# A tile for each half of attention A's values, and a later load of B's output weights

## The chip, the cores and the metric

The kernel runs on one core of one Trainium2 chip. The metric is the device time of one execution in microseconds (us); lower is better. The engines are TensorE (PE, with its weight loads as PEld), VectorE (DVE), ScalarE (ACT), GpSimd (POOL) and SyncE (SP), which here issues nearly all DMAs.

## The reference, cut to what matters

Two attentions with 32 heads of 20 columns over 2048 tokens of width 640, each followed by its output weights `wo`; the results stand side by side in the output (2048 x 1280, bf16).

```python
# A: four segments of 512 tokens, causal inside a segment, plus a memory of the segments before
for s in range(4):
    p = softmax(qs @ ks.T * scale + causal_mask)
    a_dot = p @ vs
    a_mem = (phi(qs) @ M) / (phi(qs) @ z + 1e-6)
    o = g * a_mem + (1 - g) * a_dot            # g = sigmoid(beta), one for each head
    M, z = M + phi(ks).T @ vs, z + phi(ks).sum(tokens)
a = concat(o) @ A_wo
# B: a sliding window of 256 tokens
b = softmax(where(0 <= i - j < 256, q @ k.T * scale, -1e9)) @ v
b = b @ B_wo
out = concatenate([a, b], axis=-1)
```

## The kernel before

The work is cut into eight chunks of 512 tokens, taken in turn: A0, B0, A1, B1, A2, B2, A3, B3, numbered 0 to 7. The third chunk is number 2 (A1), the fifth is number 4 (A2). For each chunk PE makes q, k and v from the transposed input `xT`, the scores of four heads at a time (`score_batch`, L814), ACT takes their exponentials (L830), POOL and DVE mask them (L869, L847), PE multiplies with the values (`av`, L883), DVE transposes the sum (L949) and POOL divides it (L987). The finished chunk goes through DRAM (`scr_o`), comes back transposed as `oT`, and PE multiplies it with the output weights `wo_A` or `wo_B` (`final_job`, L935 with tiles `wo_B,oT`).

The order of the instructions is written when the kernel is built. A model of the engines (`Flow`) keeps estimated times, and a string `PLAN` fixes the order on PE: `v20` is the first half of the values of chunk 2, `o10` the output product of chunk 1, and so on. DMAs are put on SP's queue in the order of the model's times. `load_w` enters a load with a condition and a due time; the condition `known(2, "q", 3)` holds once the model has made piece 3 of q of chunk 2. SP issues in its order and each DMA waits for what it needs, and for the eighth DMA before it.

The values of A live in one tile `vA` of 128 tokens x 4 token tiles x 696 columns. Columns 0 to 347 hold heads 0 to 15 (half 0) and columns 348 to 695 heads 16 to 31 (half 1); each head has 20 columns of values and one of ones, which sums the weights, and 12 columns of ones close each half (`HV` is 348, `at_head` gives a head's column). `v_job` makes one half: for each of the four token tiles five matmuls into a PSUM bank (L935 or L930), then one multiply on DVE that writes the tile (L733) and frees the bank. When a half is done `v_squares` copies 64 of its 128 token rows by two DMAs (L757) into the tile `vS`, shifted by 64 partitions, for the ends of the causal triangles. `dm_job` uses `vA` for the memory (L686). Dependencies are kept by tile, and where two accesses to a tile with steps may meet, the later one gets a wait.

On the start, POOL fills the ones of `vA` and `vB` (`v_ones`, L796 and L800) and zeroes `vS` (L1357).

Of the kernel before, what the change touches and what calls it, by code (L numbers as in the profile page):

```python
# [13 lines left out]
P = 128  # L14
# [70 lines left out]
def at_head(h):  # L85
    return VS * h + 12 * (h // 16)
# [181 lines left out]
class _K:  # L268
# [391 lines left out]
    def dm_job(self, seg, pkT, v):  # L660


        nc, f = self.nc, self.f
        yield self.known("pkT", seg)
        W = 4 * VS
        KT = self.KT
        spare = self.pkS
        nc.gpsimd.tensor_copy(
            out=spare[:].rearrange("p k (u r) -> p (k u) r", r=HD - DH),
            in_=pkT[:].rearrange("p k (u c) -> p (k u) c", c=HD)[:, :, DH:])  # L670
        there = f.on_pool(1000.0)
        own = [(lambda kt, m=m: pkT[:, kt, P * m:P * m + P], P, [m], m) for m in range(KT)]
        for some in (own, [(lambda kt, h=h: spare[:, kt, R2 * h:R2 * h + R2], R2,
                            [x for x in range(4) if MEM2[x][0] == h], None) for h in (1, 0)]):
            if some is not own:
                yield there
            yield "bank"
            dM, bi = self.bank()
            at = 0
            for lhs, rows, xs, g0 in some:  # L680

                gs = [g0] if g0 is not None else sorted(MEM2[x][1] for x in xs)
                n = W * len(gs)
                v0 = at_head(4 * gs[0])
                for kt in range(LT):
                    nc.tensor.matmul(dM[0:rows, at:at + n], lhsT=lhs(kt),  # L686
                                     rhs=v[:, kt, v0:v0 + n],
                                     start=(kt == 0), stop=(kt == LT - 1))
                f.on_pe("full", 4 * mm_ns(n), 4 * n, 0.0, 4)
                at += n  # L690
                if (rows, xs) != (some[-1][1], some[-1][2]):
                    yield 0.0

            rows = some[0][1]
            dv = dM[0:rows, 0:at].rearrange("p (x j c) -> p x j c", j=4, c=VS)
            if rows == P:
                mz = self.mz[:, 0:KT]
            else:
                mz = self.mz[0:rows, KT:].rearrange("p (b a) j c -> p a b (j c)", a=2)
                dv = dv.rearrange("p (a b) j c -> p a b (j c)", a=2)  # L700
            nc.vector.tensor_tensor(out=mz, in0=dv, in1=mz, op=ALU.add)
            self.close(bi, f.on_dve(100.0 + 1.04 * at, f.seen))
            f.open = False
        t = f.dve + 138.0
        yield self.known(2 * seg, "avs")
        blk, mz = self.blk, self.mz
        nc.gpsimd.tensor_tensor(out=blk[:, :, :, DH], in0=mz[:, :, :, DH], in1=self.bm[:],
                                op=ALU.mult)
        f.on_pool(150.0, t)
        nc.gpsimd.tensor_tensor(out=blk[:, :, :, 0:DH], in0=mz[:, :, :, 0:DH],  # L710
                                in1=self.ez[:].unsqueeze(3)
                                .to_broadcast([P, KT + 4, 4, DH]), op=ALU.mult)
        self.mark(f.on_pool(1700.0), "dm", seg)

    def v_job(self, n, half, w_ap, v, gate, needs):
        nc, f = self.nc, self.f
        for need in needs:
            yield need
        xT = self.xs[n]
        x0 = SH if gate else 0  # L720
        for tt in range(LT):
            yield "bank"
            ps, bi = self.bank()
            for kt in range(self.KT):
                self.wide(ps, xT[:, kt, x0 + tt * P:x0 + (tt + 1) * P],
                          w_ap[:, half, kt, :], 320, kt == 0, kt == self.KT - 1)
                if kt < self.KT - 1:
                    yield 0.0
            src = ps[:, 0:320].rearrange("p (h e) -> p h e", e=DH)
            dst = v[:, tt, HV * half:HV * half + 16 * VS].rearrange(  # L730
                "p (h e) -> p h e", e=VS)[:, :, 0:DH]
            if gate:
                nc.vector.tensor_tensor(  # L733
                    out=dst, in0=src,
                    in1=self.omg[:, 16 * half:16 * half + 16].unsqueeze(2)
                    .to_broadcast([P, 16, DH]), op=ALU.mult)
            else:
                nc.vector.tensor_copy(out=dst, in_=src)  # L738
            self.close(bi, f.on_dve(402.0, f.seen))
            f.open = False  # L740
        if not gate:
            self.v_ends(n, self.chunks[n][1], half, v)
        else:
            self.v_squares(n, half, v)
        self.used_x(n)

    def v_squares(self, n, half, v):


        f = self.f  # L750
        s = slice(HV * half, HV * half + HV)
        tok = v[0:SH, :, s].rearrange("p (a b) c -> p a b c", b=2)
        t = f.dve + 138.0

        def go():
            for odd in (0, 1):
                self.nc.sync.dma_start(  # L757
                    out=self.vS[SH * odd:SH * odd + SH, odd * 2:odd * 2 + 2, s],
                    in_=tok[:, :, odd, :])
                tl = f.on_dma(1, 410.0, t) + (1200.0 if n == 0 else 0.0)  # L760
            for g in range(4 * half, 4 * half + 4):
                self.mark(tl, n, "v", g)
        f.at(t, go)

    def v_ends(self, n, c, half, v):


        f = self.f
        lo, hi = slice(0, SH), slice(SH, P)
        s = slice(HV * half, HV * half + HV)  # L770
        todo = []
        if half == 0 and c > 0:
            pv = self.vB[(c - 1) % 2]
            todo += [(self.vU[hi, 0:2, :], pv[hi, 2:4, :], 820.0),
                     (self.vX[lo, :], pv[lo, 0, :], 410.0)]
        todo += [(self.vL[lo, :, s], v[lo, :, s], 820.0),
                 (self.vU[hi, 2:4, s], v[hi, 0:2, s], 410.0),
                 (self.vX[hi, s], v[hi, 0, s], 205.0)]
        t = f.dve + 138.0

        def go():
            for out, in_, ns in todo:
                self.nc.sync.dma_start(out=out, in_=in_)
                tl = f.on_dma(1, ns, t)
            for g in range(4 * half, 4 * half + 4):
                self.mark(tl, n, "v", g)
        f.at(t, go)

    def v_tile(self, name, now=True):
        v = self.big.tile([P, LT, VW], BF16, name=name)  # L790
# [83 lines left out]
    def av(self, parts, g, vof):  # L874
        nc, f = self.nc, self.f
        O, bi = self.bank()
        parts = sorted(parts, key=lambda e: (-e[2], e[1]))
        cols = 0
        for n_, (ref, q0, nq, c0, pts) in enumerate(parts):
            v = vof(ref)  # L880
            for j in range(4):
                h = 4 * g + j
                nc.tensor.matmul(O[HD * j:HD * j + HD, q0:q0 + nq],  # L883
                                 lhsT=v[:, at_head(h):at_head(h) + HD],
                                 rhs=pts[j // 2][:, j % 2, c0:c0 + nq],
                                 start=(n_ == 0), stop=(n_ == len(parts) - 1),
                                 tile_position=(0, HD * j), skip_group_check=True)
            cols += nq
        f.on_pe("col", cols / 2.4 + 6.0 * len(parts), cols, 0.0, 4 * len(parts))
        return O, bi  # L890
# [412 lines left out]
    def body(self, xA, A_wq, A_wk, A_wv, A_wo, A_beta, xB, B_wqkv, B_wo, out2d):  # L1303
# [39 lines left out]
        self.vL = big.tile([P, LT, VW], BF16, name="vL")  # L1343
        self.vU = big.tile([P, LT, VW], BF16, name="vU")
        self.vX = big.tile([P, VW], BF16, name="vX")
        self.vA = self.v_tile("vA")
        self.vS = big.tile([P, LT, VW], BF16, name="vS")
        self.consts_mz()
        nc.vector.memset(self.vL[:].bitcast(F32), 0.0)
        for t in (self.vU, self.vX):  # L1350
# [3 lines left out]
        nc.gpsimd.memset(self.kB[0][:, :, 0:SH], 0.0)  # L1354
        nc.gpsimd.memset(self.kB[0][:, KT:G, L:XC], 0.0)
        self.consts_ends()
        nc.gpsimd.memset(self.vS[:].bitcast(F32), 0.0)  # L1357
        f.on_pool(10500.0)
        f.on_dve(4500.0)
        k = len(self.loads)  # L1360
# [8 lines left out]
                                   None, 22000.0)  # L1369
        wo = {}  # L1370
        wo["A"] = self.load_w("wo_A", A_wo, self.known(0, "scored"), 6000.0)
        wo["B"] = self.load_w("wo_B", B_wo[0], self.known(2, "q", 3), 6000.0)

        wo["end"] = self.load_w("wo_end", B_wo[1], self.known(NC - 1, "q", KT - 1), 9000.0,
                                self.wt["wk_A"][:].rearrange("p m k c -> p (m k c)").rearrange(
# [191 lines left out]
    def one_group(self, n, kind, c, g, what, parts, left, o_t, groups_done, scro, wo, out2d):  # L1567
# [3 lines left out]
        def vof(ref):  # L1571
            what, u = ref
            if what == "a":
                return self.vA[:, u, :]
            if what in "st":
                return self.vS[:, 2 * (u % 2) + u // 2, :]
            if what == "l":
                return self.vL[:, u % LT, :]
            if what == "u":
                return self.vU[:, u + 2, :]  # L1580
            if u == 0:
                return self.vX[:]
            return self.vB[c % 2][:, u, :] if u > 0 else self.vB[(c - 1) % 2][:, LT + u, :]
# [128 lines left out]
```

## Time and profile before

| what | us |
|---|---|
| median of 3 runs | 332.24 |
| lowest and highest run | 330.19, 332.38 |
| the profiled execution's own time | 332.54 |
| its span, first to last instruction | 330.7 |
| PE, ACT, POOL, DVE busy | 316.4, 299.6, 265.4, 255.8 |
| DVE's multiplies that write vA (L733), 32 | 0.48 each |
| DMAs vS<-vA (L757), 16 | 87 KB each |
| loads of wo_B (L319), 2 | 400 KB each, issued at 73.2 |
| PE's first product with wo_B | starts at 149.6 |

All times in the text are from the start of the span of the profiled execution. A queue such as SPq lists when an engine issues a DMA, not when it lands. A wait is written "engine, line, what it works on <- what ended the wait". PE's granted clock was 1.00 throughout.

### The profile page before, as it was taken

The numbers are of one execution on the slowest core, as the hardware profiler recorded it, in microseconds if no ns is written. First come the engines' busy times: TensorE is split into PE (matmuls) and PEld (weight loads), VectorE is DVE, ScalarE is ACT, GpSimd is POOL, SyncE is SP. The second block draws the span as 40 slices with busy tenths as digits, with TensorE's granted clock in tenths as the row PEclk, the third lists the DMA queues.
The fourth block names the chain that finished last, engine by engine and source line by source line (L and its number), as shares of the span: only waits on it lengthen the run. The fifth ranks groups of instructions, "written<-read, shape, count | busy, mean of one in ns | idle before, by whom it ended". The sixth has DMA issues, their size and how long they took to land.

```text
span 330.7 us, 16968 instructions
## 1 busy us (share of the span) xinstructions
PE 316.4 (96%) x7195; PEld 176.2 (53%) x7195; DVE 255.8 (77%) x533; ACT 299.6 (91%) x333; POOL 265.4 (80%) x672
## 2 busy tenths in 40 slices
PE   7999999998999999999999999999999999999984
PEld 2454546555445455646653546456654445666652
DVE  6777767797977787999867897988777798876753
ACT  1979999998999998989999999899999999979962
POOL 8466679997759899976886999998975899989850
PEclk9999999999999999999999999999999999999999
DMA  7975945675589354165689146117868027397642
GB/s 210 388 250 135 194 138 108 150 193 159 135 214 217 67 115 132 22 141 147 138 216 174 33 86 157 50 32 154 147 181 186 14 54 185 107 233 159 109 127 80
DMA packets 76266, 47.45 MB, mean 143 GB/s; under 512 B 48382, under 2 KB 73182, under 8 KB 76190
## 3 DMA queue, kind: packets, MB, share of 16 engines
q1 hardware_dynamic: 75469, 45.71, 57.7%
q8 instruction: 56, 0.92, 1.2%
q10 hardware_dynamic: 720, 0.66, 0.7%
q14 instruction: 21, 0.16, 0.2%
HBM read 17.62 MB, written 16.96 MB: 105 GB/s over the span
## 4 chain that ended last, share of the span: by engine, by line
PE 36%; DVE 5%; ACT 3%; DMA 2%; POOL 2%; issue 1%; SPq 1%; ACTq 0%; DVEq 0%
PE m L935 19%; PE sc L814 7%; PE m L883 5%; ACT pt L830 3%; PE m L930 2%; DVE tt L949 2%; PE m L904 1%; DMA xT<-scr_o 1%; DVE pt L847 1%; DMA scr_o<-o 1%; POOL pt L869 1%; DVE kA L557 1%; POOL o L987 1%; DVE ot L1099 0%; PE m L686 0%
## 5 line engine op out<-in xcount | busy, mean ns | idle before, releaser
L830 ACT ACTIVATE pt<-sc 128x1024 bf16<-128x1024 f32 (+2 forms) x306 | 282.9, 1026 | 15.1 <-PE sc L814 12.9
L869 POOL TENSOR_SCALAR_AFFINE_SELECT pt<-pt 128x128 bf16<-128x128 bf16 (+1 forms) x512 | 178.0, 376 | 49.8 <-ACT pt L830 42.8
L949 DVE STREAM_TRANSPOSE tt<-m 128x512 f32<-128x512 f32 x88 | 61.2, 709 | 24.7 <-PE m L883 15.9
L987 POOL TENSOR_TENSOR o<-tt,rr 128x320 bf16<-128x320 f32 x64 | 48.5, 758 | 4.7 <-DVE rr L977 3.9
L814 PE MATMUL sc<-qB,kB 20*64 20x64 bf16 (+2 forms) x1728 | 39.9, 217 | 0.8 <-ACT pt L830 0.3
L935 PEld LDWEIGHTS <-xT 128*128 128x128 bf16 x296 | 26.7, 97 | 18.4 <-issue 6.1
L847 DVE TENSOR_TENSOR pt<-pt,ends 128x1024 bf16<-128x1024 bf16 (+2 forms) x50 | 36.4, 739 | 0.0
L1099 DVE CAST ot<-m 128x320 bf16<-128x320 f32 x58 | 28.1, 486 | 9.8 <-PE m L935 8.4
L814 PEld LDWEIGHTS <-kB 20*64 20x64 bf16 (+1 forms) x1728 | 22.2, 98 | 22.4 <-issue 20.5
L814 PE MATMUL sc<-qA,kA 20*64 20x64 bf16 (+4 forms) x1024 | 33.5, 237 | 0.5 <-ACT pt L830 0.4
L935 PEld LDWEIGHTS <-oT 128*128 128x128 bf16 x244 | 21.5, 97 | 12.5 <-issue 3.3
L814 PEld LDWEIGHTS <-kA 20*128 20x128 bf16 (+1 forms) x1024 | 13.4, 97 | 22.4 <-issue 21.3
L935 PE MATMUL m<-wBv,xT 128*128 128x320 bf16 x147 | 24.2, 299 | 0.9 <-DVE tt L949 0.4
L883 PE MATMUL m<-pt,vA 128*32 128x192 bf16 (+3 forms) x512 | 23.6, 274 | 0.2
L935 PE MATMUL m<-wo_A,oT 128*128 128x320 bf16 x125 | 21.0, 300 | 0.8 <-DVE kA L557 0.8
L935 PE MATMUL m<-xT,wBq 128*128 128x512 bf16 x82 | 21.4, 380 | 0.3 <-DVE tt L949 0.3
L935 PE MATMUL m<-xT,wBk 128*128 128x512 bf16 x81 | 20.7, 381 | 0.0
L935 PE MATMUL m<-wv_A,xT 128*128 128x320 bf16 x119 | 20.0, 300 | 0.2 <-DVE vA L733 0.2
L738 DVE CAST vB<-m 128x320 bf16<-128x320 f32 x32 | 15.6, 488 | 5.4 <-PE m L935 3.1
L935 PE MATMUL m<-wo_B,oT 128*128 128x320 bf16 x109 | 18.6, 300 | 0.8 <-DVE tt L949 0.4
L557 DVE CAST qB<-m 128x512 bf16<-128x512 f32 x20 | 13.8, 688 | 6.7 <-PE m L930 3.4
L935 PE MATMUL m<-xT,wk_A 128*128 128x512 bf16 x69 | 17.7, 379 | 1.2 <-DMA xT<-in_A_x_dram 1.1
(127 smaller groups left out, 460.2 us busy)
## 6 DMA issues: line engine op xcount, KB each, us to landing
out_dram<-ot SPq DMA_DIRECT2D x29, 160.0 KB
scr_o<-o SPq DMA_DIRECT2D x28, 160.0 KB
xT<-in_B_x_dram SPq DMA_DIRECT2D x8, 288.0 KB
xT<-in_A_x_dram SPq DMA_DIRECT2D x8, 256.0 KB
scr_pk<-e SPq DMA_DIRECT2D x15, 128.0 KB
vS<-vA SPq DMA_DIRECT2D x16, 87.0 KB
vL<-vB SPq DMA_DIRECT2D x8, 174.0 KB
scr_kA<-kA SPq DMA_DIRECT2D x16, 60.0 KB
```

Source lines behind the costliest of these rows:

```text
L557: nc.vector.tensor_copy(out=dst[:, m, at:at + L], in_=ps[:, :])
L738: nc.vector.tensor_copy(out=dst, in_=src)
L814: nc.tensor.matmul(ps[j // 2][h0:h1, j % 2, c0:c0 + nq], lhsT=k[rows, g, k0:k0 + h1 - h0], rhs=q[rows, g, q0:q0 + nq], start=True, stop=Tr ...
L830: nc.scalar.activation(out=pt[:, :, lo:hi], in_=ps[i][:, :, lo:hi], func=ACT.Exp, scale=self.scale)
L847: nc.vector.tensor_tensor(out=blk, in0=blk, in1=self.ends[:, c0, :].unsqueeze(1).unsqueeze(1) .to_broadcast([P, 2, n // SH, SH]), op=ALU.mult)
L869: nc.gpsimd.affine_select(out=blk, in_=blk, pattern=pat, compare_op=ALU.is_ge, fill=self.zero, base=base, channel_multiplier=mul)
L883: nc.tensor.matmul(O[HD * j:HD * j + HD, q0:q0 + nq], lhsT=v[:, at_head(h):at_head(h) + HD], rhs=pts[j // 2][:, j % 2, c0:c0 + nq], start= ...
L930: self.nc.tensor.matmul(ps[s, 0:n], lhsT=lhsT[:, s], rhs=rhs, start=start, stop=stop, tile_position=(0, HD * j), skip_group_check=True)
L935: self.nc.tensor.matmul(ps[:, 0:n], lhsT=lhsT, rhs=rhs, start=start, stop=stop, skip_group_check=True)
L949: self.nc.vector.transpose(out=tt[:], in_=O[:, :])
L987: nc.gpsimd.tensor_tensor(out=to[:] if add_to else to, in0=a, in1=b, op=ALU.mult)
L1099: nc.vector.tensor_copy(out=ot[:, 320 * hf:320 * hf + 320], in_=ps[:, 0:320])
```

## The change

`vA` and `vS` become lists of two tiles, one for each half of the heads, with 348 columns each; every reader takes the tile of its half and the column inside it. The copies keep their shape. POOL fills and zeroes two smaller tiles in place of each large one. The load of `wo_B` gets a later condition: q of chunk 4 in place of q of chunk 2. On PE, ACT and DVE the order of the instructions stays the same; on POOL three memsets of `vA` become four and one of `vS` two; on SP the two loads of `wo_B` move from before the copies `vS<-vA` of half 0 of chunk 2 to behind the last input loads of chunk 5, ahead of the stores `scr_o` of chunk 3.

```diff
@@ dm_job
-                v0 = at_head(4 * gs[0])
+                v0 = at_head(4 * gs[0]) - HV * (gs[0] // 4)
...
-                                     rhs=v[:, kt, v0:v0 + n],
+                                     rhs=v[gs[0] // 4][:, kt, v0:v0 + n],
@@ v_job
-            dst = v[:, tt, HV * half:HV * half + 16 * VS].rearrange(
+            own, c0 = (v[half], 0) if gate else (v, HV * half)
+            dst = own[:, tt, c0:c0 + 16 * VS].rearrange(
@@ v_squares
-        s = slice(HV * half, HV * half + HV)
-        tok = v[0:SH, :, s].rearrange("p (a b) c -> p a b c", b=2)
+        tok = v[half][0:SH].rearrange("p (a b) c -> p a b c", b=2)
...
-                    out=self.vS[SH * odd:SH * odd + SH, odd * 2:odd * 2 + 2, s],
+                    out=self.vS[half][SH * odd:SH * odd + SH, odd * 2:odd * 2 + 2, :],
@@ new
+    def half_tiles(self, name):
+        return [self.big.tile([P, LT, HV], BF16, name="%s%d" % (name, x)) for x in range(2)]
@@ av
-                h = 4 * g + j
+                at = at_head(4 * g + j) - (HV * (g // 4) if ref[0] in "ast" else 0)
...
-                                 lhsT=v[:, at_head(h):at_head(h) + HD],
+                                 lhsT=v[:, at:at + HD],
@@ body
-        self.vA = self.v_tile("vA")
-        self.vS = big.tile([P, LT, VW], BF16, name="vS")
+        self.vA = self.half_tiles("vA")
+        for t in self.vA:
+            nc.gpsimd.memset(t[:, :, 0:16 * VS].rearrange("p t (h e) -> p t h e", e=VS)[
+                :, :, :, DH], 1.0)
+            nc.gpsimd.memset(t[:, :, HV - 12:HV], 1.0)
+        self.vS = self.half_tiles("vS")
...
-        nc.gpsimd.memset(self.vS[:].bitcast(F32), 0.0)
+        for t in self.vS:
+            nc.gpsimd.memset(t[:].bitcast(F32), 0.0)
...
-        wo["B"] = self.load_w("wo_B", B_wo[0], self.known(2, "q", 3), 6000.0)
+        wo["B"] = self.load_w("wo_B", B_wo[0], self.known(4, "q", 0), 6000.0)
@@ one_group, vof
-                return self.vA[:, u, :]
+                return self.vA[g // 4][:, u, :]
...
-                return self.vS[:, 2 * (u % 2) + u // 2, :]
+                return self.vS[g // 4][:, 2 * (u % 2) + u // 2, :]
```

## The prediction

> **What bounds the kernel now.** I read the busy shares first. TensorE (PE) is busy 96% of the span of 330.7 us and runs one fixed order of instructions, so whatever it idles in the middle of the kernel is lost; ScalarE (ACT) has 91%, VectorE (DVE) 77%.
>
> ```profile
> PE 316.4 (96%) x7195; PEld 176.2 (53%) x7195; DVE 255.8 (77%) x533; ACT 299.6 (91%) x333; POOL 265.4 (80%) x672
> ```
>
> PE therefore has 14.3 us of idle time in all. Busy time by stretches of 20 us says where: 2.0 us lie before 20 us, 5.6 us after 312 us, and the largest loss in between is 2.0 us from 72 to 92 us, in the third chunk (the second of attention A).
>
> ```profile
> 60.00:72.00 12.00, 11.99 (x277) 6.45 (x273) 10.59 (x23) 11.44 (x14) 11.86 (x28) 1.00 0.72 180
> 72.00:92.00 20.00, 18.00 (x387) 9.95 (x389) 16.93 (x39) 18.51 (x23) 14.71 (x34) 1.00 0.59 149
> ```
>
> The columns are the stretch, its length, then busy time of PE, PEld, DVE, ACT and POOL, the granted clock (1.00 throughout), the share of the DMA engines and GB/s. The waits inside that stretch name the cause:
>
> ```profile
> PEld L883 <- DVE vA L733: 1.5, 1, 1.5
> DVE vA L733 <- DMA vS<-vA: 1.5, 1, 1.5
> PE m L883 <- DVE vA L733: 1.0, 1, 1.0
> ...
> PE m L935 <- DVE kA L557: 0.8, 2, 0.5
> ...
> PE m L935 <- DVE vA L733: 0.2, 1, 0.2
> ```
>
> DVE stands for 1.5 us before one write of values (L733) because a DMA still reads that tile, and PE stands 1.0 us for DVE, then 0.8 and 0.2 us for DVE work behind it. The timelines of the three queues put times to it (start, length, engine, line):
>
> ```profile
> 71.44 1.67 SPq L651 DMA_DIRECT2D scr_pk<-e  x2
> 73.17 2.07 SPq L319 DMA_DIRECT2D wo_B<-in_B_wo_dram  x2
> 75.33 1.33 SPq L757 DMA_DIRECT2D vS<-vA  x2
> 76.75 1.76 SPq L509 DMA_DIRECT2D scr_qA<-qA  x4
> ```
>
> ```profile
> 77.51 0.52 DVE L598 TENSOR_TENSOR pq<-pq,e 128x512 bf16<-128x512 bf16 x1
> 79.51 0.49 DVE L733 TENSOR_TENSOR vA<-m,omg 128x320 bf16<-128x320 f32 x1 [1.49 <-DMA vS<-vA]
> ```
>
> ```profile
> 78.44 0.62 PE L930 MATMUL m<-xT,wk_A 128*32 128x512 bf16 x8
> 80.06 0.29 PE L883 MATMUL m<-pt,vX 128*32 128x256 bf16 x4 [1.01 <-DVE vA L733]
> ```
>
> SP issues the 800 KB of wo_B at 73.17, and the copies vS<-vA of heads 0 to 15 behind them at 75.33; they have landed when DVE goes on at 79.51. What DVE then writes is vA of heads 16 to 31, which those copies don't read: one tile holds both halves.
>
> The chain of waits from the end reaches back only to 163 us, so it doesn't itself say that this stall sets the end. I take it to do so because PE's order is fixed and, between 88 and 163 us, PE waits on no DMA at all: each of its waits there is 0.3 us or less, on DVE, ACT, POOL or issue, whose work PE itself feeds.
>
> **The change part by part.**
>
> *Two tiles for vA.* With a tile to each half, L733 for heads 16 to 31 waits for its matmul alone; the order of the instructions shows the DMA wait gone there. The matmul had ended (wv_A,xT x5 from 76.68 for 0.85 us, so 77.5), so L733 starts when DVE is free, at 78.02 instead of 79.51: 1.49 us. Walked on: PE gets its bank 1.01 us earlier (it was free at 79.05). DVE is then busy without a gap until past 85.1, so its cast kA (L557) moves from 81.18 to 79.69, after its matmul's end at 79.06; PE, which waited 0.47 us for it until 81.91, gets there at 80.43 and finds it done at 80.42. PE is now 1.48 us ahead. The waits of 0.36 us (85.15) and 0.16 us (86.15) stay, since DVE and PE moved alike. ACT idled 0.93 us at 81.0 for the same cast and 0.50 us at 86.9 for PE: it can follow by 1.43 us. POOL idled 1.32 us before 80.25 for DVE and 0.38 us at 82.5, enough to follow. I take 1.45 us. Lower bound: 1.01 us, only PE's wait on L733. Upper bound: 2.0 us, all four waits.
>
> It is the only wait of the kind that cost anything: over the whole trace the line "DVE vA L733 <- DMA" counts one. The other removed waits and their semaphore steps (21 ns each, at most 14) I cost at nothing: below 0.3 us on an engine that is 77% busy.
>
> *DVE against POOL.* In the stretch that moves, the multiply pq (L598) took 0.91 us at 80.35, beside POOL's o (L987) from 80.25 for 0.73 us, and 0.42 us at 82.80. The Trainium skill, SBUF — State Buffer, section Who interferes with whom, says that a VectorE instruction with two SBUF inputs and a GpSimd instruction that reads SBUF exclude each other, and that the one to issue second blocks. By it the 0.49 us depends on who is first: DVE would reach L598 at 78.86 and POOL its o no earlier than 78.93, so DVE would win and the gain would be some 1.9 us; were the old order kept, it stays at 1.45 us. One such pair can't settle it; the sum keeps 1.45 us.
>
> *vS as two tiles.* Still 16 copies of 87 KB with rows of the same length; no change. The reads by PE (L883, L686) keep shapes and count: no change.
>
> *POOL's fills at the start.* One memset of vA's ones (0.67 us) and two of its ends (0.51 us) become four, vS's 1.25 us becomes two halves. By the small memsets (0.10 us for one element) that adds 0.1 to 0.3 us. POOL ends them at 7.94 and idles 2.34 us until 10.28 for ACT, so nothing shows; uncovered it would be those 0.3 us.
>
> *wo_B out of the third chunk.* Two issues (2.07 us on SP) and 819 KB leave. At the 240 GB/s of 75 to 79 us those bytes are 3.4 us of transfers ahead of vS and scr_qA. SP's next instruction, vS, waits for L733 of the same half (ended 75.48), so SP gains little there. But scr_qA and the loads qA behind it (81.26) come some 1 to 2 us sooner. No PE or ACT wait in that stretch names those DMAs, so this alone is worth nothing more. It overlaps with the first part: with vS no longer behind wo_B, the copies would land some 1.5 to 3 us sooner, and most of the 1.49 us would go by this edit alone. The two gains don't add up.
>
> *wo_B into the fifth chunk.* By the order of instructions the two issues now come on SP after the loads xT of 125.39 (which end at 127.02) and before scr_o:
>
> ```profile
> 125.39 1.63 SPq L355 DMA_DIRECT2D xT<-in_B_x_dram  x2
> 138.68 2.49 SPq L1021 DMA_DIRECT2D scr_o<-o  x4
> ```
>
> ```profile
> 131.00:135.00 4.00, 3.98 (x117) 2.35 (x116) 3.61 (x7) 3.34 (x4) 3.83 (x7) 1.00 0.00 0
> 135.00:139.00 4.00, 3.85 (x106) 2.10 (x112) 3.76 (x9) 3.99 (x6) 4.00 (x10) 1.00 0.02 4
> ```
>
> ```profile
> 149.64 1.53 PE L935 MATMUL m<-wo_B,oT 128*128 128x320 bf16 x10
> ```
>
> SP waits for DVE in between, and the DMA engines do nothing from 131 to 139. Issue takes 0.4 to 1.6 us each, the transfer 3.4 us, so wo_B lands near 134, some 14 us before PE's first use even when that comes 1.45 us earlier (148.2). The queue behind it (scr_o, then vS at 141.28) isn't ready before 137. Cost: nothing. Without that cover it would be the 3.4 us.
>
> **Sum.** 0 + 1.45 + 0 + 0 + 0 = 1.45 us less. The profiled execution took 332.54 us (span 330.7 and 1.8 around it): 331.1. The median of the runs, 332.24, is 0.3 lower, so the prediction is 330.8 us, 0.4% less. A difference up to 1%, 3.3 us, is about what a measurement of this kernel can't tell from none; the three runs of before alone span 330.19 to 332.38.
>
> **The rivals.**
>
> *The gain is lost again* (the time stays at 332.2). ACT, at 91%, becomes the bound after 88 us, or a later wait takes up the 1.45 us. For it: the chain doesn't reach back to 80 us, and DVE is busy 4.00 of 4.00 us from 139 to 143 with PE waiting on it. Against it: ACT's own waits are mostly on PE's scores (12.9 us, 23 times), so ACT follows PE. 0.20.
>
> *More than the stall* (329.8 or lower). All four PE waits go (2.0 us), the pq multiply wins its port (0.5 us), total 2.5 us and 329.8. For it: DVE is the neck from 79 to 87 us. Against it: 0.36 and 0.16 us wait on work that moves along with PE. 0.17; the part of it below 328.9 needs a further 0.9 us that no row shows.
>
> *wo_B comes too late* (slower). The place is PE's first m<-wo_B,oT at 149.64. From the point where wo_B lands after 148.2 PE stands still. If SP got to it only behind the copies, stores and loads of the fifth chunk, which it issues from 141.28 to 153.3, then 2.1 us of issue and 3.4 us of transfer put it at 158.8: 10.6 us of stall, and 341 us if nothing of it is won back. Against it: the order puts the issues before 138.68, and 14 us lie between. 0.05. A smaller loss (333 to 335, a tuned order that meets other timings of DMA) gets 0.05.
>
> *The wait doesn't go.* L733 could have been waiting for something else that the profile laid on the DMA. Against it: its matmul ended at 77.5 and DVE was free at 78.02. 0.03, with 332.2.
>
> **How the numbers follow.** The forecast itself, 330.3 to 331.6, has 0.50. Faster by over 1% (under 328.9) is part of the second rival and of plain scatter (the lowest run of before less 1.45 is 328.7): 0.16. Slower by over 1% is the late wo_B and a little of the scatter: 0.08. The rest, 0.76, is within 1%. The range runs from the lowest run of before less 1.45 us, 328.7, to 332.8, the time unchanged plus half a microsecond.
>
> **What would show it.** Right: no wait of L733 on vS<-vA, the write of the third chunk's second half within 0.1 us of DVE's multiply before it, PE busy at least 19.3 of the 20 us from 72 to 92, wo_B's issues near 127 with no PE wait at its first use, and every later landmark (the first m<-wo_B,oT at 149.64) 1.2 to 1.7 us earlier. Wrong: that landmark is early but the end is not (lost later), PE's wait at 80 us remains under another name, or a wait "PE m L935 <- DMA wo_B" appears.

## The result, and the profile after

| | median | runs from .. to | profiled execution | its span |
|---|---|---|---|---|
| before | 332.42 us | 329.65 .. 336.27 (22 runs) | 332.54 us | 330.7 us |
| after | 330.28 us | 329.28 .. 333.09 (22 runs) | 331.96 us | 330.2 us |

The ratio of after to before is 0.9945, with a 95% interval of 0.9926 to 0.9963. That is 1.8 us less (0.55% of 332.4), between 1.2 and 2.5 us: a small gain, but one that the interval keeps apart from none. The profiled execution of after is one of its slower ones, 1.7 us above its median; its span is only 0.5 us shorter than that of before, and where the rest went is read below. Medians and ranges here and below hold every execution; the ratios leave out those more than 1.5% above the fastest of their kernel.

In the busy time by stretches (stretch, length, then PE, PEld, DVE, ACT, POOL, granted clock, DMA share, GB/s) the third chunk of after is fuller, and less data moves beside it:

```profile
60.00:72.00 12.00, 11.83 (x285) 6.41 (x272) 10.70 (x23) 11.44 (x14) 11.86 (x28) 1.00 0.77 191
72.00:92.00 20.00, 18.76 (x465) 11.03 (x467) 18.18 (x41) 19.47 (x25) 15.59 (x37) 1.00 0.52 122
```

The waits of PE in that stretch are these. Its 1.0 us on `vA` (before on L733, now L734) is gone:

```profile
PE m L939 <- issue: 0.4, 1, 0.4
PE m L939 <- DVE kA L557: 0.3, 1, 0.3
PE sc L818 <- ACT pt L834: 0.2, 1, 0.2
PE m L939 <- DVE vA L734: 0.2, 1, 0.2
```

The timeline of DVE shows the write of heads 16 to 31 at 78.40 without a wait, right on the end of the multiply before it (78.48); before, it stood at 79.51. The next two-input multiply `pq` still takes 0.92 us:

```profile
78.05 0.43 DVE L598 TENSOR_TENSOR pq<-pq,e 128x512 bf16<-128x512 bf16 x1
78.40 0.48 DVE L734 TENSOR_TENSOR vA<-m,omg 128x320 bf16<-128x320 f32 x1
...
79.22 0.92 DVE L598 TENSOR_TENSOR pq<-pq,e 128x512 bf16<-128x512 bf16 x1
```

SP's queue has `wo_B` in the fifth chunk, and the view of that tile shows PE's first use at 148.3, 22 us behind the end of the issues, with no wait on the DMA:

```profile
124.21 1.91 SPq L319 DMA_DIRECT2D wo_B<-in_B_wo_dram  x2
137.36 2.49 SPq L1025 DMA_DIRECT2D scr_o<-o  x4
```

```profile
L939 PE MATMUL m<-wo_B,oT x109: 296/299/310, 148.3 to 306.3; 128*128 128x320 bf16 x109
```

To see what becomes of a gain, PE's weight loads of two traces can be laid side by side, since their number (7195) and order are the same: the lead is how much earlier the same one starts. In this execution the lead is 0 at 70 us, 1.12 at 80 to 90, 1.31 at 100 to 150, 1.2 until 250, 0 at 253 and 0.06 at 290. One instruction takes it, by a stop of PE for which the profile names nothing but issue:

```profile
251.48 0.33 PE L818 MATMUL sc<-qA,kA 20*128 20x320 bf16 x4
252.84 0.26 PE L818 MATMUL sc<-qA,kA 20*128 20x192 bf16 x4 [1.03 <-issue]
```

So the lead reached 250 us, and was lost there to something else. Whether that belongs to the change or to this one execution is a question for the experiments.

### The profile page after: what moved, and what is told of

Its sections match the earlier page's. It is cut to its first block, busy times and chain, and to the rows that moved or that the text cites. A ratio compares the mean times of both kernels' runs of the same rounds, so it can differ in the third digit from the quotient of the medians.

```text
span 330.2 us, 16932 instructions
## 1 busy us (share of the span) xinstructions
PE 313.6 (95%) x7160; PEld 176.4 (53%) x7195; DVE 255.8 (77%) x533; ACT 299.7 (91%) x333; POOL 266.0 (81%) x674
## 4 chain that ended last, share of the span: by engine, by line
PE 63%; POOL 10%; DVE 9%; ACT 8%; issue 4%; DMA 4%; SPq 1%; ACTq 0%; DVEq 0%; POOLq 0%
PE m L939 33%; PE sc L818 12%; PE m L887 9%; PE m L934 7%; ACT pt L834 7%; POOL pt L873 6%; DVE tt L953 4%; DVE pt L851 1%; POOL o L991 1%; DMA xT<-in_A_x_dram 1%; DMA xT<-scr_o 1%; PE m L908 1%; DVE ot L1103 1%; PE m L686 1%; DMA scr_o<-o 1%
## 5 line engine op out<-in xcount | busy, mean ns | idle before, releaser
L939 PE MATMUL m<-xT,wBq 128*128 128x512 bf16 x73 | 20.6, 380 | 0.8 <-DVE tt L953 0.3
L939 PE MATMUL m<-xT,wBk 128*128 128x512 bf16 x70 | 19.6, 380 | 0.7 <-issue 0.3
L557 DVE CAST kB<-m 128x512 bf16<-128x512 f32 x20 | 13.6, 680 | 6.6 <-PE m L939 5.6
```

Source lines behind the costliest of these rows:

```text
L557: nc.vector.tensor_copy(out=dst[:, m, at:at + L], in_=ps[:, :])
L939: self.nc.tensor.matmul(ps[:, 0:n], lhsT=lhsT, rhs=rhs, start=start, stop=stop, skip_group_check=True)
```

## The experiments

The theory: L733 waited for copies that `wo_B`'s 800 KB held up on the same queue, and that share a tile with what it writes only by name. Either part of the change alone removes that; both do not give more; the lead is carried to the end, less what stops on issue take in a single execution. The rivals: only the tiles matter (the wait was on the tile, whatever the traffic); or the gain is that of the bytes, so that it moves with the place of `wo_B`; or the fifth chunk has a price of its own. The experiments are in three groups: the two parts (e1, e2, e3, e4), the third and fifth chunk (e5 to e8), and single executions for the late stops (e9 to e12).

**e1: the changed kernel once more**

> The changed kernel once more, for a second profile beside the parts. Theory (the 1.5 us that DVE waited for vS<-vA at 78 us went to the end): 1.5 to 2.1 us under the kernel before, DVE, ACT and PE some 1.1 to 1.5 us earlier from 80 us to the end, and no stop of PE of 1 us on issue near 252 us, which would then belong to the one execution profiled. Rival (the stall at 252 us belongs to the change, the earlier PE meets a transpose by DMA there): PE stops for 0.8 to 1.2 us near 252 us again and the lead is back under 0.3 us behind it.

Measured: 330.84 us (330.17 to 332.67, 12 runs) against 332.75; ratio 0.9942, from 0.9913 to 0.9971. Profiled execution 330.17, span 328.4. Here three of PE's four waits of the third chunk are gone, the fourth, of 0.16 us, is down to 0.11, and a new one of 0.40 us has come, on ACT, which has two exponentials of 1.0 us in a row just there. The timelines of PE, ACT, DVE and POOL:

```profile
79.89 0.68 PE L818 MATMUL sc<-qB,kB 20*64 20x64 bf16 x62 [0.40 <-ACT pt L834]
```

```profile
78.76 2.00 ACT L834 ACTIVATE pt<-sc 128x1024 bf16<-128x1024 f32 x2
```

```profile
77.68 0.48 DVE L734 TENSOR_TENSOR vA<-m,omg 128x320 bf16<-128x320 f32 x1
...
78.59 0.43 DVE L598 TENSOR_TENSOR pq<-pq,e 128x512 bf16<-128x512 bf16 x1
```

```profile
78.69 0.91 POOL L991 TENSOR_TENSOR o<-tt,rr 128x320 bf16<-128x320 f32 x1
```

DVE's `pq` starts 0.10 us ahead of POOL's `o`, takes 0.43 us, and POOL's takes 0.91. In the first profile of after it was the other way round: POOL's started at 79.13 and took 0.73, `pq` at 79.22 and took 0.92. The lead of PE is 0.26 at 70 us (this execution started that much sooner), 1.66 at 80, 1.86 at 90, 2.16 at 100 and 1.81 at 310: it stays. The stop of 1.0 us near 252 isn't there.

**e2: the tiles alone (`wo_B` stays in the third chunk)**

```diff
 # from the kernel after
-        wo["B"] = self.load_w("wo_B", B_wo[0], self.known(4, "q", 0), 6000.0)
+        wo["B"] = self.load_w("wo_B", B_wo[0], self.known(2, "q", 3), 6000.0)
```

> The tiles for each half alone; wo_B is loaded in the third chunk as before. Theory (either part alone takes the same wait away): no wait of L734 on vS<-vA, 1.2 to 2.1 us under before, within 0.4 us of both parts together. Rival (the lighter DMA queue of the third chunk is the gain): under 0.6 us of gain, the rest only with the later load.

Measured: 332.89 us (329.29 to 334.04) against 332.75; ratio 0.9970, from 0.9933 to 1.0008: by the time alone, unclear. The profile says more. PE's lead is 0.38 at 70 us, 1.77 at 80, 2.14 at 100 and still 1.54 at 290, nearly as much as in e1. Then all of it and more is lost in one place, in the timeline of PE and in the busy time by stretches (columns as above):

```profile
292.25 0.61 PE L818 MATMUL sc<-qB,kB 20*64 20x64 bf16 x53
294.92 0.32 PE L818 MATMUL sc<-qB,kB 20*64 20x64 bf16 x11 [2.06 <-issue]
```

```profile
290.00:292.00 2.00, 2.00 (x74) 1.45 (x72) 1.33 (x3) 1.30 (x2) 2.00 (x6) 1.00 1.05 281
...
294.00:296.00 2.00, 1.08 (x15) 0.67 (x16) 0.00 (x0) 0.72 (x1) 0.79 (x2) 0.69 0.86 238
296.00:298.00 2.00, 2.00 (x23) 0.94 (x22) 1.09 (x2) 1.22 (x2) 0.00 (x0) 0.50 0.31 72
298.00:300.00 2.00, 2.00 (x31) 1.19 (x28) 1.47 (x3) 1.85 (x3) 0.76 (x2) 0.96 0.21 42
```

A stop of 2.06 us on issue, and then 3.4 us at a granted clock of 0.50, in which a product with `wo_A` (x5) takes 1.51 us in place of 0.84. A stop of 0.86 us at 305 takes another 1.0 us of lead. The stall of the third chunk is gone with the tiles alone, then; in the execution profiled, the time was lost again by stops 200 us later. That the same made the kernel's other slow executions is likely but not shown, since they have no trace.

**e3: the later load alone (one tile as before)**

```diff
 # from the kernel before
-        wo["B"] = self.load_w("wo_B", B_wo[0], self.known(2, "q", 3), 6000.0)
+        wo["B"] = self.load_w("wo_B", B_wo[0], self.known(4, "q", 0), 6000.0)
```

> The later load of wo_B alone; vA and vS stay one tile each. Theory (either part alone): vS<-vA of the third chunk, no longer behind 800 KB, lands near 77.8 us, so the wait of L733 falls from 1.5 to 0 to 0.3 us, and the time is 1.0 to 2.0 us under before. Rival (copies need their 2.8 us whatever is ahead of them, only the tiles help): the wait stays 0.8 us or more and the gain is under 0.7 us.

Measured: 331.17 us (329.27 to 333.71) against 332.75; ratio 0.9954, from 0.9923 to 0.9985. The tile is whole, and still the write waits for nothing, because the copies are no longer behind 800 KB (SP's queue, then DVE):

```profile
74.30 1.72 SPq L757 DMA_DIRECT2D vS<-vA  x2
```

```profile
77.49 0.45 DVE L598 TENSOR_TENSOR pq<-pq,e 128x512 bf16<-128x512 bf16 x1
77.86 0.48 DVE L733 TENSOR_TENSOR vA<-m,omg 128x320 bf16<-128x320 f32 x1
```

The copies are issued at 74.3 and 75.4 in place of 75.3 and 76.1, so the queue of issues is part of it; the rest of the 1.5 us must be a shorter way from issue to landing, which the trace doesn't give for these two. The lead grows by 1.39 us between 70 and 80, as in e1 and e2. Either part alone takes the whole stall; the rival that only the tiles matter is out.

**e4: more bytes ahead of the copies.** The kernel before with a second 800 KB, from `wo_B`'s input into scratch DRAM, entered beside it; it adds work that the reference doesn't need.

```diff
 # from the kernel before
+        self.load_w("wo_spare", B_wo[0], self.known(2, "q", 3), 6000.0,
+                    self.dram.tile([P, 2, KT, D // 2], BF16, name="wo_spare"))
```

> The kernel before with another copy of wo_B's 800 KB, into scratch memory that nobody reads, issued behind the loads of wo_B: half of it ahead of vS<-vA, half behind scr_qA<-qA. It asks whether a longer wait of DVE at 78 us reaches the end one for one. Theory: the wait of L733 grows from 1.5 to 3.0 to 4.0 us and the time by 1.4 to 2.5 us. Rival (a later wait takes it up, the stall isn't on the path that sets the end): the wait grows as much and the time by under 0.6 us.

Measured: 334.70 us (332.70 to 338.52) against 332.75; ratio 1.0058, from 1.0024 to 1.0091. Only half of the new bytes came ahead of the copies; the second issue went out at 79.90:

```profile
73.14 1.88 SPq L319 DMA_DIRECT2D wo_B<-in_B_wo_dram  x2
75.07 0.60 SPq L319 DMA_DIRECT2D wo_spare<-in_B_wo_dram  x1
75.76 1.36 SPq L757 DMA_DIRECT2D vS<-vA  x2
```

The waits from 72 to 92 us, and the busy time by stretches behind them:

```profile
DVE vA L733 <- DMA vS<-vA: 2.7, 1, 2.7
PE m L883 <- DVE vA L733: 2.2, 1, 2.2
```

```profile
82.00:84.00 2.00, 1.96 (x91) 1.45 (x79) 2.00 (x6) 0.91 (x1) 1.69 (x5) 0.50 0.67 234
...
85.00:87.00 2.00, 1.98 (x19) 1.01 (x18) 1.91 (x5) 1.09 (x3) 0.73 (x2) 1.00 0.57 91
```

The wait grew from 1.49 to 2.66 us by 400 KB more, less than the 3.0 to 4.0 us expected: the more bytes ahead, the longer it is. PE fell 1.17 us behind by 80, and 1.54 by 90, with the clock at 0.50 for 3.4 us behind the stop of 2.17. A delay in this place reaches the end as a lead does: PE is still 1.3 us late at 150 (and 2.7 at 290, after further stops).

**e5, e6: the tiles alone again, and the values' tiles alone.** e5 is the kernel of e2. In e6 `vA` is split, `vS` is one tile, and `wo_B` stays in the third chunk.

```diff
 # e6, from the kernel of e2
-        self.vS = self.half_tiles("vS")
+        self.vS = big.tile([P, LT, VW], BF16, name="vS")
...
-                    out=self.vS[half][SH * odd:SH * odd + SH, odd * 2:odd * 2 + 2, :],
+                    out=self.vS[SH * odd:SH * odd + SH, odd * 2:odd * 2 + 2, HV * half:HV * half + HV],
...
-                return self.vS[g // 4][:, 2 * (u % 2) + u // 2, :]
+                return self.vS[:, 2 * (u % 2) + u // 2, :]
```

> The tiles for each half alone, once more, with wo_B in the third chunk. Its first profile kept the lead of 1.5 us to 290 us and lost it there to a stop of PE of 2.06 us on issue, with the granted clock at 0.50 for 3.4 us behind it. Theory (that stop is a chance of the execution, as likely with either place of wo_B): 1.2 to 2.1 us under before, and no stop of 1 us behind 280 us in the profile, or one elsewhere. Rival (the load of wo_B in the third chunk sets the later transfers so that the stop comes in most executions): 0 to 1 us under before, and a stop of 1 us or more on issue between 280 and 310 us again.

> Two tiles for vA only; vS stays one tile and wo_B is loaded in the third chunk. Theory (the wait comes from vA alone, written while a copy reads it): no wait of L734 on vS<-vA, and the same time as with both tiles split, within 0.6 us. Rival (vS counts too): a wait of 0.3 us or more at the copies or at PE's reads of vS, and 0.5 us or more over the kernel with both split.

Measured: e5 331.45 us (329.09 to 335.67) against 332.99, ratio 0.9948, from 0.9914 to 0.9982; e6 331.22 us (329.65 to 335.70) against the same, ratio 0.9960, from 0.9932 to 0.9988. Both profiled executions keep the lead to the end (spans 328.1 and 327.9), and the third chunk with `wo_B` in it is as full as without (e5):

```profile
72.00:92.00 20.00, 19.33 (x471) 11.16 (x470) 17.45 (x40) 19.85 (x24) 16.01 (x38) 1.00 0.64 168
```

e2's late stop was therefore not a fixed price of that kernel. Splitting `vS` adds nothing that shows.

**e7, e8: `wo_B` early, and as late as it may come.** Both have the split tiles. In e7 the load follows that of `wo_A` at 45.8 us; in e8 it stands behind the copies of the fifth chunk.

```diff
 # from the kernel after: e7
-        wo["B"] = self.load_w("wo_B", B_wo[0], self.known(4, "q", 0), 6000.0)
+        wo["B"] = self.load_w("wo_B", B_wo[0], self.known(0, "scored"), 9000.0)
 # e8
-        wo["B"] = self.load_w("wo_B", B_wo[0], self.known(4, "q", 0), 6000.0)
+        wo["B"] = self.load_w("wo_B", B_wo[0], self.known(4, "q", 3), 6000.0)
```

> Both tiles split; wo_B is loaded behind wo_A in the second chunk, near 46 us. Theory (the place of wo_B matters only by what it delays; here nothing that PE waits for): 1.3 to 2.1 us under before, as with the load in the fifth chunk. Rival (the empty stretch of the DMA engines from 128 to 137 us is what makes the later load good): under 1.0 us of gain, with PE waiting on a regrouping of kB or qB near 56 us or on issue.

> Both tiles split; wo_B is loaded later in the fifth chunk, behind the copies vS<-vA of half 0 near 142 us instead of ahead of scr_o near 124 us. It prices the case of wo_B coming too late. Theory: issued near 142, landed 147 to 150, against a first use at 148.3: PE waits 0 to 2 us for wo_B there, and the time is 0.3 to 2 us over the changed kernel. Rival (PE's order leaves enough room even there): no wait of PE on wo_B and the time of the changed kernel within 0.4 us.

Measured, against the 332.99 of e5: e7 331.38 us (329.06 to 333.68), ratio 0.9953, from 0.9918 to 0.9988; e8 330.66 us (329.08 to 333.60), ratio 0.9942, from 0.9910 to 0.9975. In e8 SP and the tile `wo_B` show:

```profile
139.36 1.65 SPq L757 DMA_DIRECT2D vS<-vA  x2
141.05 1.33 SPq L319 DMA_DIRECT2D wo_B<-in_B_wo_dram  x2
```

```profile
L939 PE MATMUL m<-wo_B,oT x109: 296/299/310, 147.7 to 305.6; 128*128 128x320 bf16 x109
```

Even 6.6 us from issue to first use was enough, and no PE wait names that DMA; of the wait and the longer time that were expected, neither came. From 46 to 141 us the place of `wo_B` makes no difference that these intervals could tell. The rival of the bytes as such is out.

**e9 to e12: single executions.** e9, e10 and e11 are the kernel of e2 again, e12 is the kernel before.

> The tiles for each half alone, a look for its profile. In 13 of its 24 timed executions this kernel took 331.9 us or more, against 4 of 34 with wo_B in the fifth chunk; one such execution is profiled. Theory (PE's own supply of instructions fails once or twice in such an execution, at places with much DMA): where the profiled time is over 331.9, PE shows a stop on issue of 0.8 us or more, perhaps with the granted clock at 0.50 behind it, and the lead gained at 78 us is whole until there; where it is under 331, no such stop beyond 1.3 us in all. Rival (the wait at 78 us comes back in another form): a time over 331.9 with PE late between 72 and 92 us.

> As the look before it: the same kernel, and the same two answers, in another execution.

> As the two looks before it: the same kernel, and the same two answers, in another execution.

> The kernel before, for a second profile. Theory: the wait of DVE on vS<-vA near 78 us is there again with 1.0 to 2.0 us, and PE busy 17.5 to 18.6 of the 20 us from 72 to 92. Rival (the wait was a chance of the one execution profiled): under 0.5 us.

Measured, one time each: 331.49, 330.24, 331.97, and 333.31 for before (another execution of before beside them took 334.42). The wait at 78 us is gone in e9 to e11. The theory of the late stops holds in part: e10 has no stop on issue longer than 0.2 us, but e11, at 331.97, has none of the 0.8 us expected, only one of 0.52 at 242 and one of 0.62 at 294, and e9 has three, of 0.58, 0.26 and 0.26, between 205 and 243. e12 repeats the wait of the first profile, 0.25 us longer:

```profile
DVE vA L733 <- DMA vS<-vA: 1.7, 1, 1.7
```

The table has the lead of PE over the first profile of before, in us, less each execution's own lead at 70 us, at five places:

| kernel | 80 | 90 | 100 | 200 | 290 |
|---|---|---|---|---|---|
| after, first profile | 1.16 | 1.16 | 1.35 | 1.26 | 0.10 |
| e1 after again | 1.40 | 1.60 | 1.90 | 1.61 | 1.55 |
| e2 tiles alone | 1.39 | 1.58 | 1.76 | 1.45 | 1.16 |
| e3 later load alone | 1.39 | 1.59 | 1.74 | 1.07 | 0.93 |
| e5 tiles alone | 1.39 | 1.60 | 1.74 | 2.14 | 1.93 |
| e6 values' tiles alone | 1.38 | 1.59 | 1.87 | 1.84 | 1.84 |
| e7 wo_B early | 1.39 | 1.60 | 1.75 | 1.43 | 0.83 |
| e8 wo_B late | 1.40 | 1.60 | 1.82 | 1.82 | 0.86 |
| e9 tiles alone | 1.39 | 1.59 | 1.89 | 1.71 | 0.43 |
| e10 tiles alone | 1.39 | 1.60 | 1.89 | 1.87 | 1.71 |
| e11 tiles alone | 1.40 | 1.60 | 1.91 | 1.54 | 0.81 |
| e12 before again | -0.25 | -0.25 | -0.08 | -0.58 | -0.99 |
| e4 more bytes | -1.17 | -1.54 | -1.36 | -2.10 | -2.70 |

Up to 100 us ten executions without the wait agree within 0.2 us, and only the first profile of after has less. From there to 290 us they lose up to 1.5 us (e5 wins 0.2), most of it by stops on issue, at places that change from one to the next. Behind 290 e2 loses 3.1 more and e11 0.55; the kernel before loses some too (0.9 us in e12 from 100 to 290). One part stays open. Of the executions that count in the ratios, with e9 to e11, those at 331.9 us or more are 16 of 37 in the kernels without the wait but with `wo_B` in the third chunk (e2, e5, e6, e9 to e11), and 11 of 70 in those with it elsewhere (after, e1, e3, e7, e8). The late stops seem to come more often with the old place of `wo_B`; but the line of 331.9 was drawn after e2 and e5 were measured, these two, the same kernel, differ by 1.4 us in their medians, and no trace shows how a load at 73 us should matter at 293. No kernel here is clearly below the changed one.

## Why the prediction was right or wrong

*The wait goes.* Right: L734 starts within 0.1 us of the end of the multiply before it in all eleven traces without the wait, and the rival that it wouldn't go is out.

*Its size.* The sum said 1.45 us for the profiled execution. The ratio gives 1.8 (1.2 to 2.5), and the traces say where the difference is: the sum came near in part by luck, since two of its steps were off in opposite directions. The walk had PE 1.48 us ahead from 82 us on. It is 1.13 ahead from 82 to 84 us in all eleven traces (each less its own lead at 70): PE met ACT, 0.40 us in ten of them. The walk kept ACT out because ACT had idled 0.93 us there, but with PE ahead ACT's two exponentials become the neck for a moment. The other step is "the waits of 0.36 us (85.15) and 0.16 us (86.15) stay, since DVE and PE moved alike". They stayed only in the first profile of after (0.33 and 0.16), whose lead therefore stays at 1.16 up to 90 us. In e1 to e3 and e5 to e11 the first is gone and the second is 0.11 to 0.13: the lead goes to 1.55 at 85 us and to 1.58 to 1.60 at 90.

A further 0.14 to 0.30 us came between 90 and 100 us. But e4 and e12, which have the stall, gain 0.18 and 0.16 us there as well, so about that much lies in the first profile of before, against which the lead is taken, and not in the change; no wait of PE accounts for it. The stall itself differs from one execution to the next: against e12 each lead at 90 us would be 0.25 us larger, 1.85 in place of 1.60. The prediction also took a difference of up to 1% for one that a measurement of this kernel can't tell from none; 22 runs a side told 0.55% from none.

*DVE against POOL.* Those two waits shrank because `pq` won. The prediction said that one pair can't settle who pays, but the profile of before holds a second one, the other way round (DVE, then POOL):

```profile
82.80 0.42 DVE L598 TENSOR_TENSOR pq<-pq,e 128x512 bf16<-128x512 bf16 x1
```

```profile
82.93 0.88 POOL L987 TENSOR_TENSOR o<-tt,rr 128x320 bf16<-128x320 f32 x1 [0.38 <-DVE rr L977]
```

In e1 to e3 and e5 to e11 the first pair behaves like it: 0.42 to 0.43 us where `pq` starts first, with POOL's `o` at 0.91 instead of 0.73. This is what the Trainium skill, SBUF — State Buffer, section Who interferes with whom, states (the second to issue blocks), and the traces agree in both directions: 0.10 us decided who paid 0.49 and who 0.18. Whether the second stands still for all of the other's time isn't shown: POOL lost 0.18 us with 0.33 us of `pq` still to run. The prediction named the result by that rule, some 1.9 us, and the condition, but kept 1.45; ten profiles of eleven have the other branch, and reach 1.60 because of ACT. In the first profile of after the order stayed, it seems, by an accident of that execution: PE's stop of 0.41 us on issue at 73.24 made DVE's transpose start at 76.86 (76.51 before), while POOL was on time (76.84, 76.80 before).

*The gain is carried.* Right: of the leads at 100 us, 1.07 to 2.14 are there at 200, and the delay of e4 is carried in the same way. The reason given, that PE's order is fixed and ACT follows, fits but wasn't tested by itself, and at 80 us ACT did hold PE up. "The gain is lost again" came true in some executions: wholly in the profiled one of after and in e2, for the most part in e9 and e11. It came by a mechanism that the prediction didn't have: neither ACT nor a later wait, but stops on issue, of 1.03 us at 252 in the first of these and 2.06 at 293 in the second.

*More than the stall.* The mechanism was right in half: three of the four waits went and `pq` won, but PE met ACT, and the sum of 2.0 and 0.5 counted most of one time twice: the waits of 0.36 and 0.16 us are there where `pq` is slow, and gone or down to 0.11 where it is fast, so 0.4 of their 0.52 us are the 0.49 us of `pq` as PE meets it.

*wo_B in the fifth chunk.* Cost nothing, as said; it was issued at 124.2, not near 127, and first used at 148.3, 1.3 us earlier. In the third chunk the loads of `qA` came 0.3 us (after) to 0.8 us (e3) sooner, not 1 to 2; nothing on PE or ACT waited for them, as said. The slower rival, 341 us for an issue behind the loads of 153.3, had its nearest test in e8: issued at 141.05 `wo_B` still came in time.

*The two gains don't add up.* Right: e3 and e5 each have what e1 has.

*PE busy at least 19.3 of the 20 us.* Wrong in the first profile (18.76), just missed in e1 to e3 (19.27 to 19.28) and right in e5 to e11 (19.33 to 19.50). The figure fits the sum: 18.00 and 1.45 are 19.45. The first profile missed it by what the walk didn't have, 0.41 us on issue and 0.18 on ACT, beside the 0.33 and 0.16 us that stayed.

## What to carry to other kernels

When a write waits for a DMA that reads the same tile, look at which bytes each of them touches and at what stands ahead of that DMA in its queue: here either cure, a tile to each half or the bulk load elsewhere, was worth the whole stall, and both together no more. After a stall is taken out, walk on to the next engine that gets work sooner, and ask of each pair of neighbours who now comes first. And before a late loss is read as the price of a change, look at a second execution: the lead of one engine's instructions over the same ones before tells a loss in one place from a gain that never came.

## What the runs showed of the hardware

A stop of PE can have a second price. Behind the stop of 2.06 us in e2 (292.87 to 294.92) and the wait of 2.17 us in e4 (79.03 to 81.20) the granted clock was 0.50 for 3.4 us; behind 1.01 us in before, 1.03 us in after and 1.25 us in e12 it stayed at 1.00. The Trainium skill, TensorE: Matmul & The Clock Gate, Part 1: The HAM clock gate (the "warmup" mystery), says that the gate watches activity in windows of about 3.4 us, halves the clock after an idle one and gives it back after a busy one; the length of the slow stretch agrees, while these stops, at some 2.1 us, were shorter than such a window and were enough.

What causes the stops on issue isn't shown. Ahead of the one in e2 the DMA engines of the core are busy all the time (share 1.05 from 290 to 292).
